# Three score blocks and four value blocks per visit of the tensor engine, in a fused attention, Fourier-mixing and FFN kernel

## The chip, the cores and the metric

The kernel runs on one core of one Trainium2 chip. The metric is the device time of one execution in microseconds (us), as the median over runs of the same program. TensorE is called PE below (its weight loads PEld), VectorE is DVE, ScalarE is ACT, GpSimd is POOL and SyncE is SP; "L509" is line 509 of the kernel before.

## The reference

Eight batches, twelve heads, 448 positions, 64 channels a head. The attention has no softmax: the scores are passed through a squared relu. Its output goes through two Fourier transforms whose real part is added to it, a layer norm, and an FFN with residual.

```python
scores = scale * np.matmul(q, k.transpose(0, 1, 3, 2))
attn = np.maximum(scores, 0.0) ** 2 / S
x = np.matmul(attn, v)                      # (B, H, S, D) -> (B, S, H * D)
X = np.fft.fft(np.fft.fft(x, axis=1), axis=2)
u = x + np.real(X)
un = (u - mean(u)) / np.sqrt(var(u) + 1e-06)
out = u + np.maximum(un @ w_ch1, 0.0) @ w_ch2
```

## The kernel before, in words

**Work per batch.** Two heads make one channel tile m of 128 channels, six tiles a batch (MC = 6). The 448 keys are cut in four blocks of 112. One score block (L509) is two matmuls, one per head: each contracts over 64 channels, on its own half of the array's rows, and writes 112 x 448 scores into one half of a two-bank PSUM tile psS. ACT takes the relu of such a tile into a bfloat16 tile sq (L541), DVE squares it in place (L536), and one value block (L525) is two matmuls, one per head, each into its own 64 partitions of a one-bank tile psT. Four value blocks accumulate in one psT; then DVE reads it twice (the two scaled copies into xT, L431 and L438) and makes the sum and the difference of its halves (L446, L447, and from the fourth tile on L456, L458). So a batch has 24 score blocks and 24 value blocks.

**The rest of a batch.** The folded tiles go through the channel transform (L815, 24 matmuls), are cast by ACT and DVE (L827), go through the sequence transform (L677, 8 matmuls), and become the rows u and the normalised rows un (L688 to L723 on ACT, DVE and POOL). u and un are stored to DRAM, and un comes back transposed as unT (L762). The FFN of a batch then has an up phase (L905: 24 groups of six matmuls, each group into one bank psF, relu into hT by ACT at L895, in the first batch every second one by DVE at L893) and a down phase (L940: groups of 24 matmuls into one bank psF, the residual added by DVE at L922). The FFNs take 384 and 512 rows in turn, so a matmul of the up phase streams 384 or 512 columns; a down phase has 144 or 192 matmuls of 384 columns.

**PSUM.** The eight banks are: two tiles psS of two banks each (tag S), two tiles psT of one bank (tag T) and two psF of one bank (tag F). psS also serves the transforms, psF the transposes of q and k in the first two batches (L409) and the warm-up matmuls (L959).

**What sets the order.** `Streams.run` writes the whole program in one pass on the host. Every part of the kernel is a generator that asks with `need(engine, duration, dependencies, buffers, ok)` for its next piece of work; the planner holds a clock per engine, from cost formulas (`mm`, `act`, `dve`, `dve2`, `SWITCH`, `LATENCY`), and gives the engine to the piece that can start first, and among equals to the lower rank. The lists `BS`, `BT` and `BF` hold the times at which the banks of the tags S, T and F come free by that clock. On the chip each engine then executes its instructions strictly in the written order and waits where an operand or a buffer isn't there. An attention of batch b may run ahead of the FFNs by `LEAD` only.

**A visit.** One turn of the loop in `attention` (L475 and after) is called a visit here: the score matmuls of G key blocks and, LAG visits later, the value matmuls of G key blocks, directly behind them in PE's order. G is 1 for the first two batches and 2 after that. The relus of the scores and the squares are asked for by the same generator, so the next visit is asked for when these have been placed. In the FFN likewise, the relu of a group is placed after the next group of matmuls was, by the same generator (`pend`).

**Other queues.** POOL issues the loads of q, k, v and of the weights, and SP the transposes and stores. The copies of q and k at L379 on DVE have one buffer each, which the transposing DMAs at L388 have to have read before the next copy.

## Time and profile before

| | before |
|---|---|
| median of three runs (lowest to highest) | 640.99 us (640.28 to 646.23) |
| the profiled execution: its time / its span from first to last instruction | 641.72 us / 639.8 us |
| busy PE / PEld | 618.9 us / 322.3 us |
| busy DVE / ACT / POOL | 332.6 us / 319.9 us / 126.7 us |
| granted clock of PE, mean over the span | 0.991 |
| DMA, mean | 131 GB/s |

The page of the profile gives busy time per engine, the chain of work that ended last, the costliest groups of instructions and the transfers. In a row of the groups, "x192 | 167.7, 916 | 135.0" means 192 instructions, busy 167.7 us together, 916 ns each on average, and 135.0 us in which the engine stood idle just before one of them. Busy time counts an instruction from its start to its modelled end, and neighbouring matmuls overlap; what a run of matmuls costs is therefore read from the chain of work, which gives the time from a piece's start to the next one's.

### The profile page before, as it was taken

To read this page: it belongs to the slowest core of one execution; us is meant where nothing else is said; L and a number is where in the kernel's file an instruction comes from. 1 tells how busy PE (TensorE), PEld (TensorE's weight loads), DVE (VectorE), ACT (ScalarE), POOL (GpSimd) and SP (SyncE) were. 2 spreads that over 40 slices of the span, in tenths; PEclk is the share of its full clock that TensorE was granted. 3 is DMA by queue.
4 is the path that set the end of the run, shared out by engine and by line. 5 is a ranking of instruction groups with operands and counts; after the bars stand their busy time and mean duration, and the time that the engine had idled before them with its cause. 6 is when DMAs were issued, how large, how long until landed. Compare 5 with 4: busy or idle time off the path is not lost.

```text
span 639.8 us, 10069 instructions
## 1 busy us (share of the span) xinstructions
PE 618.9 (97%) x3923; PEld 322.3 (50%) x3938; DVE 332.6 (52%) x763; ACT 319.9 (50%) x471; POOL 126.7 (20%) x176
## 2 busy tenths in 40 slices
PE   8997999899999999999999999999999999999997
PEld 5464445344544556444544556444544556554464
DVE  6866777676456435765366434765275435410011
ACT  6956752655575245754475245754575334404300
POOL 8342033311331103220241103311040002300000
PEclk9998999899999999999999999999999999999999
DMA  9999999688648658696547767698336213531021
GB/s 120 203 207 228 218 126 224 177 122 142 118 143 146 132 98 157 150 180 112 101 147 135 142 113 133 145 207 114 73 129 137 65 60 90 145 113 44 0 78 72
DMA packets 128688, 83.91 MB, mean 131 GB/s; under 512 B 79504, under 2 KB 116512, under 8 KB 128640
## 3 DMA queue, kind: packets, MB, share of 16 engines
q0 software_dynamic: 40512, 34.64, 33.7%
q1 hardware_dynamic: 88128, 48.63, 32.2%
q8 instruction: 31, 0.51, 0.4%
q14 instruction: 17, 0.14, 0.1%
HBM read 62.91 MB, written 27.60 MB: 141 GB/s over the span
## 4 chain that ended last, share of the span: by engine, by line
PE 80%; DVE 6%; ACT 6%; DMA 4%; issue 2%; SPq 1%; POOL 0%; DVEq 0%; ACTq 0%; POOLq 0%
PE psF L940 34%; PE psF L905 28%; PE psT L525 7%; PE psS L509 7%; ACT sq L541 3%; DMA unT<-nbot 2%; DMA qkT<-qkr 1%; PE psS L815 1%; DVE stats L709 1%; PE psS L677 1%; ACT un L723 1%; DVE u L698 1%; PE psS L506 1%; PE psS L791 1%; PE psF L959 1%
## 5 line engine op out<-in xcount | busy, mean ns | idle before, releaser
L541 ACT ACTIVATE sq<-psS 112x896 bf16<-112x896 f32 x192 | 167.7, 916 | 135.0 <-PE psS L509 134.7
L905 PE MATMUL psF<-unT,w 128*128 128x384 bf16 (+1 forms) x1137 | 229.0, 352 | 2.8 <-DVE hT L893 1.4
L940 PE MATMUL psF<-w,hT 128*128 128x384 bf16 x1344 | 229.4, 327 | 0.3 <-ACT hT L895 0.3
L940 PEld LDWEIGHTS <-hT 128*128 128x128 bf16 x1344 | 127.7, 98 | 100.4 <-issue 20.0
L905 PEld LDWEIGHTS <-w 128*128 128x128 bf16 x1152 | 109.2, 98 | 111.7 <-issue 15.9
L895 ACT ACTIVATE hT<-psF 128x512 bf16<-128x512 f32 (+1 forms) x180 | 98.3, 547 | 109.6 <-PE psF L905 106.9
L536 DVE TENSOR_TENSOR sq<-sq 112x896 bf16<-112x896 bf16 x192 | 113.3, 618 | 30.1 <-ACT sq L541 29.8
L922 DVE TENSOR_TENSOR o<-psF,o 128x384 f32<-128x384 f32 x56 | 31.2, 556 | 144.8 <-PE psF L940 144.7
L509 PE MATMUL psS<-qkT 64*112 64x448 bf16 x384 | 63.2, 380 | 6.0 <-ACT sq L541 6.0
L293 POOL DMA_DIRECT2D vn<-in_v_dram x24 | 17.4, 724 | 216.5 <-PE psT L525 216.5
L525 PE MATMUL psT<-sq,vn 112*64 112x448 bf16 x384 | 59.4, 371 | 0.2 <-DVE sq L536 0.2
L431 DVE TENSOR_SCALAR xT<-psT 128x224 bf16<-128x224 f32 x48 | 18.7, 390 | 53.4 <-PE psT L525 53.4
L509 PEld LDWEIGHTS <-qkT 64*112 64x112 bf16 x384 | 20.5, 125 | 41.8 <-issue 40.6
L697 POOL TENSOR_TENSOR u<-tp,xn 128x385 f32<-128x385 f32 (+1 forms) x14 | 14.5, 1033 | 116.0 <-DVE tp L688 109.8
L525 PEld LDWEIGHTS <-vn 112*64 112x64 bf16 x384 | 15.5, 108 | 33.6 <-issue 33.3
L723 ACT ACTIVATE un<-u,nmr,rstd 128x768 bf16<-128x768 f32 (+1 forms) x28 | 27.9, 1022 | 3.8 <-DVE nmr L718 3.7
L709 DVE BATCH_NORM_STATS2 stats<-u 128x6 f32<-128x384 f32 (+1 forms) x56 | 27.7, 534 | 0.0
L739 POOL DMA_INDIRECT ubot<-u,back x16 | 16.0, 1002 | 30.3 <-ACT sq L541 25.0
L739 POOL DMA_INDIRECT nbot<-un,back x15 | 14.5, 969 | 37.4 <-ACT un L723 32.4
L959 PE MATMUL psF<-warm 128*128 128x256 bf16 x114 | 18.9, 303 | 1.1 <-DVE warm L205 1.1
L827 DVE CAST pc<-psS 97x772 bf16<-97x772 f32 x8 | 8.2, 1030 | 20.8 <-PE psS L815 20.0
L438 DVE TENSOR_SCALAR xT<-psT 128x224 bf16<-128x224 f32 x47 | 18.1, 386 | 0.0
(122 smaller groups left out, 372.9 us busy)
## 6 DMA issues: line engine op xcount, KB each, us to landing
out_dram<-o SPq DMA_DIRECT2D x28, 384.0 KB
vn<-in_v_dram POOLq DMA_DIRECT2D x24, 224.0 KB, 5.2
qn<-in_q_dram POOLq DMA_DIRECT2D x21, 224.0 KB, 6.6
kn<-in_k_dram POOLq DMA_DIRECT2D x21, 224.0 KB, 8.3
w<-in_moe_w_ch_dram POOLq DMA_DIRECT2D x12, 384.0 KB, 13.5
w<-in_moe_w_ch_dram POOLq DMA_DIRECT2D x4, 1152.0 KB, 26.8
utop<-u SPq DMA_DIRECT2D x8, 384.0 KB
o<-utop SPq DMA_DIRECT2D x8, 384.0 KB
```

The source lines that it names most:

```text
L509: nc.tensor.matmul(sc[:R, h, 0:S].rearrange("k (c q) -> k c q", c=4), lhsT=kT[ps, m % 2, c, :], rhs=qT[ps, m % 2], start=True, stop=True)
L525: nc.tensor.matmul(av[h * Dh:(h + 1) * Dh, 0:S], lhsT=vn[:, c, h0 + h, :], rhs=sq[:, h, :], start=(c == 0), stop=(c == 3))
L536: nc.vector.tensor_tensor(r, r, r, op=ALU.mult)
L541: nc.scalar.activation(r, sc[:R, :, 0:S], AF.Relu)
L709: nc.vector.bn_stats(stats[:n, hf, :], u[:n, hf * (D // 2):(hf + 1) * (D // 2)])
L723: nc.scalar.activation(un[:n], u[:n], AF.Identity, bias=nmr[:n, i:i + 1], scale=rstd[:n, i:i + 1])
L739: nc.gpsimd.indirect_dma_start(out=bot, out_offset=bass.IndirectOffsetOnAxis(ap=back[ch][:s1 - s0], axis=0), in_=us[1][:s1 - s0], in_offse ...
L895: nc.scalar.activation(h[:, 0:N], ph[:, 0:N], AF.Relu)
L905: nc.tensor.matmul(ph[:, 0:N], lhsT=w1_sb[m][hf][:, jj * 128:(jj + 1) * 128], rhs=unT[:, m, 0:N], start=(m == 0), stop=(m == MC - 1))
L922: nc.vector.tensor_tensor(o[:, hs], pc[:, 0:D // 2], o[:, hs], op=ALU.add)
L940: nc.tensor.matmul(pc[:, 0:D // 2], lhsT=hT[j][:, c * 128:(c + 1) * 128], rhs=w2_sb[j // 6][:, j % 6, hs], start=(j == 0), stop=(j == JC - 1))
L959: nc.tensor.matmul(pw[:, 0:256], lhsT=warm[:, 0:128], rhs=warm, start=True, stop=True)
```

## The change

- **PSUM**: three tiles psS of two banks (tags S0 to S2) and two banks psF (F0, F1). The tag T is gone. A class `Banks` gives each tile a tag of its own and hands out the one that came free first. The values are collected in a bank psF; the warm-up matmuls and the last of the first batch's row tiles move from psF to psS.
- **A visit** issues the values first, all four key blocks of a channel tile at once (eight matmuls), once their squares belong to the scores issued a visit earlier (three visits earlier in the first batch and until the first FFN begins), and then the scores of three key blocks (six matmuls), one block in the early part. A visit may have only one of the two.
- **Streams of their own**: the relu of the scores (`squares`), each square (`square`), the relu of an FFN group (`relu`), the reloading of the residual (`reload`) and the residual add with its store (`add`) are generators that the planner places by themselves.
- **SBUF**: nine tiles sq instead of six, one tile xn instead of two.

```diff
+class Banks(Bufs):
+    def __init__(self, n, make):
+        super().__init__(n)
+        self.make, self.ids, self.tiles = make, [(0.0, i) for i in range(n)], {}
+    def take(self):
+        first = min(self.ids)
+        self.ids.remove(first)
+        t = self.make(first[1])
+        self.tiles[id(t)] = t, first[1]
+        return t
+    def give(self, t, when):
+        self.free.append(when)
+        self.ids.append((when, self.tiles.pop(id(t))[1]))
...
-        return psum.tile([128, 2, 512], FP32, name="psS", tag="S", bufs=2)
...
-    BS, BT, BF = Bufs(2), Bufs(2), Bufs(2)
+    BS = Banks(3, lambda i: psum.tile([128, 2, 512], FP32, name="psS", tag=f"S{i}", bufs=1))
+    BF = Banks(2, lambda i: psum.tile([128, 512], FP32, name="psF", tag=f"F{i}", bufs=1))
...
-    BSQ = Bufs(6)
+    NSQ = 9
+    BSQ = Bufs(NSQ)
...
-    BXN = Bufs(1)
+    BXN = Bufs(0)
...
-        BT.free.append(e1 - 2 * dve2(NS))
+        BF.give(av, e1 - 2 * dve2(NS))
...
-        G, LAG = (1, 3) if b < 2 else (2, 2)
-        NP = 4 * MC // G
...
+        while pa < NB:
+            few = b == 0 or progress[0] == 0.0
+            n = min(1 if few else 3, NB - p)
+            ma = pa // 4
+            lag = 3 if few else 1
+            old = fresh[-lag] if len(fresh) >= lag else 0
+            values = pa + 4 <= old if n else True
+            n = max(0, min(n, NSQ - (p - pa - 4 * values)))
+            values = values or not n
+            fresh.append(p + n)
             deps, bufs, dur = [], [], 0.0
+            if values:
+                deps += [sqs[i][1] for i in range(pa, pa + 4)]
+                bufs.append(BF)
...
+            if n:
+                deps += [turned_at[b][i // 8][i // 4 % 2] for i in (p, p + n - 1)]
+                bufs += [BS] * n
...
+            if scs:
+                sch.add(squares(scs, sqs), (0.2, 0.2))
             if av_end is not None:
                 yield from fold(b, ma, F, av, av_end)
+
+    def squares(scs, sqs):
+        for i, sc, t in scs:
+            e = yield need("ACT", act(2 * S) - 0.03, [t + LATENCY["PE"]], [BSQ])
+            r = sqs[i][0] = work.tile([R, 2, S], BF16, name="sq", tag="sq", bufs=NSQ)
+            nc.scalar.activation(r, sc[:R, :, 0:S], AF.Relu)
+            BS.give(sc, e + 0.1)
+            sch.add(square(r, e + LATENCY["ACT"], sqs[i][1]), (0.2, 0.2))
+
+    def square(r, t, done):
+        e = yield need("DVE", dve2(2 * S), [t])
+        nc.vector.tensor_tensor(r, r, r, op=ALU.mult)
+        done.t = e + LATENCY["DVE"]
...
-                if pend:
-                    yield from relu()
-                pend = (ph, e, j)
-                if j in (JC // 2, JC // 2 + 2):
-                    yield from reload()
...
+            sch.add(relu(ph, e, j), (0, 0))
+            if j in (JC // 2, JC // 2 + 2):
+                sch.add(reload(j // 2 - JC // 4), (4, 0))
...
-                        if jq == 0 and pend:
-                            yield from add()
-                    pend = (pc, e, c, half)
-            yield from add()
...
+                sch.add(add(pc, e, c, half), (0, 0))
```

**What moves in the order.** On PE, in the down phase of the third FFN (144 matmuls of 384 columns): psF are the FFN's groups, psS scores, psT values; of every run of like matmuls only the first row is shown. Before:

```order
L940 MATMUL psF_3302<-w2_0_811,hT_2936 128x384
...
L509 MATMUL psS_3334<-qkT_2690 112x448
...
L525 MATMUL psT_3340<-sq_3076,vn_2620 64x448
...
L940 MATMUL psF_3302<-w2_3_879,hT_3222 128x384
...
L509 MATMUL psS_3375<-qkT_2690 112x448
...
L525 MATMUL psT_3340<-sq_3316,vn_2620 64x448
...
L940 MATMUL psF_3359<-w2_2_856,hT_3126 128x384
```

The same place with the change, where a visit takes the values (L524) ahead of the scores (L542):

```order
L959 MATMUL psF_3405<-w2_0_798,hT_2956 128x384
...
L524 MATMUL psF_3455<-sq_3349,vn_2824 64x448
...
L542 MATMUL psS_3464<-qkT_2923 112x448
...
L959 MATMUL psF_3447<-w2_1_822,hT_3091 128x384
...
L542 MATMUL psS_3529<-qkT_2923 112x448
...
L959 MATMUL psF_3508<-w2_3_849,hT_3285 128x384
```

Before, the runs have 18, 4, 4, 18, 4, 4 and 12 matmuls; with the change 30, 8, 6, 36, 6 and 36. The runs have become longer and fewer, and the second visit shown has no values.

Counted over the whole of PE's order from the first FFN group on, these are the runs of like matmuls that lie between others:

| runs on PE from the first FFN group on | before | with the change |
|---|---|---|
| of scores (322 matmuls) | 89 | 54 |
| of values (328 matmuls) | 91 | 41 |
| of FFN matmuls, up and down (2496) | 122 | 91 |

With the change 26 of the score runs of six lie in up phases and 27 in down phases, and 21 of the value runs in up phases and 20 in down phases. Ahead of the first FFN group there are 62 score and 56 value matmuls in both orders, in 31 and 27 runs before, in 28 and 7 with the change, and 142 and 152 warm-up matmuls.

On ACT, in the up phase of the third FFN, sq is the relu of one score block and hT that of one FFN group. Before:

```order
L541 ACTIVATE sq_2925<-psS_2913 112x896
L895 ACTIVATE hT_2936<-psF_2906 128x384
L541 ACTIVATE sq_2938<-psS_2916 112x896
L895 ACTIVATE hT_2956<-psF_2929 128x384
L895 ACTIVATE hT_2965<-psF_2945 128x384
L895 ACTIVATE hT_2974<-psF_2958 128x384
```

With the change, at the sixteenth group of the same up phase:

```order
L562 ACTIVATE sq_3238<-psS_3213 112x896
L920 ACTIVATE hT_3248<-psF_3224 128x384
L562 ACTIVATE sq_3254<-psS_3216 112x896
L920 ACTIVATE hT_3264<-psF_3241 128x384
L920 ACTIVATE hT_3266<-psF_3256 128x384
L562 ACTIVATE sq_3276<-psS_3219 112x896
```

A visit in an up phase now puts three relus of scores among those of the FFN's groups.

On PE in the up phase of the third FFN, the bank of the values. Before, psT lies beside psF:

```order
L905 MATMUL psF_2929<-unT_2515,w1_0_0_341 128x384
...
L525 MATMUL psT_2976<-sq_2874,vn_2194 64x448
...
L905 MATMUL psF_2984<-unT_2515,w1_0_0_341 128x384
...
L525 MATMUL psT_2976<-sq_2925,vn_2194 64x448
...
L905 MATMUL psF_3028<-unT_2515,w1_0_0_341 128x384
```

With the change the values take one of the two psF:

```order
L943 MATMUL psF_3224<-unT_2631,w1_0_1_427 128x384
...
L524 MATMUL psF_3290<-sq_3023,vn_2564 64x448
...
L542 MATMUL psS_3299<-qkT_2734 112x448
...
L943 MATMUL psF_3323<-unT_2631,w1_0_1_427 128x384
...
L524 MATMUL psF_3363<-sq_3254,vn_2564 64x448
```

From the values' first matmul until DVE has read their bank, the FFN has one bank of the two.

More of the change, by code (lines that the diff above doesn't have):

```diff
@@ L564, in first_rows @@
         n = s1 - s0
-        BP = [BS, BT, BS, BF][2 * ch + i]
+        BP = BF if (ch, i) == (0, 1) else BS
         e = yield need("PE", 8 * mm(D // 2) + 6 * 0.06, [pcs[0][1], pcs[1][1]] + x_ready[0],
-                       [BP] * (1 + i))
-        if i:
-            pu = [(psF if ch else psT)() for _ in range(2)]
-        else:
-            pu = psS()
-            pu = [pu[:, 0], pu[:, 1]]
+                       [BP] * (2 if BP is BF else 1))
+        if BP is BF:
+            pu = held = [BF.take() for _ in range(2)]
+        else:
+            held = [BS.take()]
+            pu = [held[0][:, 0], held[0][:, 1]]
         for hf in range(2):
@@ L630, in first_rows @@
         e1, e2 = ends
-        BP.free += [e1, e2] if i else [max(e1, e2)]
+        for t, e in zip(held, (e1, e2) if BP is BF else (max(e1, e2),)):
+            BP.give(t, e)
         first_us[ch][i] = u, max(e1, e2) + LATENCY["ACT"], max(e1, e2)
@@ L958, in warming @@
             e = yield need("PE", 0.12 if e > 5.0 else 0.23, [e + gap])
-            nc.tensor.matmul(pw[:, 0:256], lhsT=warm[:, 0:128], rhs=warm, start=True, stop=True)
-        BF.free.append(e)
+            nc.tensor.matmul(pw[:, 0, 0:256], lhsT=warm[:, 0:128], rhs=warm, start=True, stop=True)
+        BS.give(pw, e)
     LEAD = 1.9
```

269 lines of the change are left out of this document (120 added, 149 removed).

## The prediction

> **What bounds the kernel now.** I first read the busy times on the page and the stage in which all FFNs but the last run.
>
> ```profile
> PE 618.9 (97%) x3923; PEld 322.3 (50%) x3938; DVE 332.6 (52%) x763; ACT 319.9 (50%) x471; POOL 126.7 (20%) x176
> 127.00:546.00 419.00, 414.39 (x2533) 209.99 (x2545) 231.09 (x530) 221.04 (x328) 76.69 (x88) 1.00 0.63 127
> ```
>
> In the second row the columns are length, then busy time of PE, PEld, DVE, ACT and POOL, granted clock, DMA share and GB/s. PE is busy for 414.4 of 419 us at full clock, DVE and ACT for little more than half of it. PE is the bound, but its busy time doesn't say what it does with the time, since overlapping matmuls are counted to their modelled ends. So I went to the waits of PE next, from 70 us on, where the columns are total, times and longest.
>
> ```profile
> PE psS L509 <- ACT sq L541: 5.8, 12, 1.7
> PE psF L905 <- DVE hT L893: 1.4, 3, 0.9
> PE psF L905 <- ACT hT L895: 0.7, 2, 0.5
> PE psF L940 <- ACT hT L895: 0.3, 2, 0.2
> ```
>
> Together 8.2 us. Waiting is not where much can be had. What is left is the chain of work, which shows what a run of matmuls costs from its start to the next run's: start, length, what. The first three rows are from the stage with one block a visit, the others from the stage with two.
>
> ```profile
> 66.80 0.33 PE psS L509 x2
> 67.13 0.31 PE psT L525 x2
> 67.44 1.08 PE psF L905 x6
> ...
> 259.41 3.09 PE psF L940 x18
> 262.50 0.52 PE psS L509 x4
> 263.01 0.50 PE psT L525 x4
> ...
> 267.56 2.06 PE psF L940 x12
> ...
> 280.90 4.01 PE psF L940 x24
> ...
> 296.28 5.29 PE psF L905 x24
> ```
>
> Two score matmuls take 0.33 us and four take 0.52: a block adds 0.19, so the run itself costs 0.33 - 0.19 = 0.14 beside its matmuls. Values: 0.31 and 0.50, again 0.19 a block and 0.12 for the run. FFN matmuls of 384 columns: 1.08, 2.06 and 4.01 us for 6, 12 and 24, so 0.98 for six and 0.10 for the run. The price belongs to the change of kind and not to the semaphore waits: each value block in a run has its own wait on DVE, and the second still adds only 0.19.
>
> **Part 1: fewer runs.** From the first FFN group on, the order has 35 score runs less (89 to 54), 50 value runs less (91 to 41) and 31 FFN runs less (122 to 91). That removes 35 x 0.14 + 50 x 0.12 + 31 x 0.10 = 4.9 + 6.0 + 3.1 = 14.0 us, with the same matmuls. A score run of six then takes 0.14 + 3 x 0.19 = 0.71 us, a value run of eight 0.12 + 4 x 0.19 = 0.88. Nothing hides this: PE is the bound there. Ahead of the first FFN group the value runs fall from 27 to 7, but there the gaps are filled with warm-up matmuls (142 before, 152 after), so a shorter run only makes room for them; I take nothing.
>
> The Trainium skill gives this price a cause and a smaller size. By "TensorEngine Tiling (Array Packing)", Key Properties, changing the tiling mode drains the array, and scores (half the rows), values (half the columns) and FFN (the whole array) are three modes; by "TensorE: Matmul & The Clock Gate", Step-by-step, draining takes some 128 cycles, which is an estimate of 0.053 us at 2.4 GHz. By that the 116 runs less would give 6.2 us, and the sum below 636.8 us instead of 629.0. The rows show 0.10 to 0.14 us for a run, so the sum goes by them.
>
> **Part 2: waits for a score tile.** Twelve waits make the 5.8 us quoted above. They lie where two visits follow one another with little between them:
>
> ```profile
> 199.19 3.34 ACT L541 ACTIVATE sq<-psS 112x896 bf16<-112x896 f32 x4 [1.35 <-PE psS L509]
> 200.16 0.40 PE L509 MATMUL psS<-qkT 64*112 64x448 bf16 x2 [0.32 <-ACT sq L541]
> 200.96 0.40 PE L509 MATMUL psS<-qkT 64*112 64x448 bf16 x2 [0.41 <-ACT sq L541]
> ```
>
> Four relus take ACT 3.34 us and PE asks for the third and fourth tile too early, 0.73 us in each batch. With the change nearly every pair of score runs has at least 18 FFN matmuls, 3 us, between them; I found one place where only six and a value run (0.98 + 0.10 + 0.88 us) stand between. Three relus take 2.75 us by the first row of part 3. I take 4 of the 5.8 us as gone; the bounds are 0 and 5.8.
>
> **Part 3: three relus among those of the FFN.** The durations, as count, busy, mean ns, and idle before:
>
> ```profile
> L541 ACT ACTIVATE sq<-psS 112x896 bf16<-112x896 f32 x136 | 117.9, 915 | 121.0 <-PE psS L509 121.0
> L895 ACT ACTIVATE hT<-psF 128x512 bf16<-128x512 f32 x92 | 55.0, 598 | 71.7 <-PE psF L905 69.6 <-issue 2.1
> L895 ACT ACTIVATE hT<-psF 128x384 bf16<-128x384 f32 x72 | 35.1, 490 | 25.6 <-PE psF L905 25.0 <-issue 0.5
> ```
>
> In an up phase the FFN has two banks; the bank of one group has to be read while PE makes the next, 0.98 us at 384 columns and 5.29 / 4 = 1.32 us at 512. A group's relu that comes just after a score relu has begun ends 0.92 + 0.49 = 1.41 us after its matmuls, or 0.92 + 0.60 = 1.52: late by 0.43 or 0.20 us. In the long run ACT has the time: a visit with three scores, four values and 18 FFN matmuls of 384 columns is 0.71 + 0.88 + 3.04 = 4.63 us of PE and 3 x 0.92 + 3 x 0.49 = 4.23 of ACT. But three relus in a row come close to that. The order has 26 such visits in up phases, where before most score runs lay in down phases. Bounds: 0 if the longer runs of PE cover it, and two late groups a visit at 384 columns, 26 x 0.86 = 22 us, above. I take 0.2 us a visit, near the lower end because the separate streams put an FFN relu between the score relus as soon as it is there: +5 us.
>
> **Part 4: the values' bank.** The two reads of a value tile, and what may stand ahead of them on DVE:
>
> ```profile
> L431 DVE TENSOR_SCALAR xT<-psT 128x224 bf16<-128x224 f32 x35 | 13.7, 392 | 48.0 <-PE psT L525 48.0
> L438 DVE TENSOR_SCALAR xT<-psT 128x224 bf16<-128x224 f32 x35 | 13.5, 385 | 0.0
> L698 DVE TENSOR_TENSOR u<-tp,xn 128x383 f32<-128x383 f32 x6 | 7.6, 1270 | 0.0
> ```
>
> Before, they held a bank psT that nobody else wanted. Now they hold one of the FFN's two, for 0.78 us behind the last value matmul. PE makes an FFN group in the other bank meanwhile, 0.98 or 1.32 us, and in most visits 0.71 us of scores too, so the usual cost is nothing. If the longest neighbour, 1.27 us, stands ahead, the bank comes free after 2.05 us, and PE has waited 0 to 1.07 us. In a down phase a bank is filled for 4 us and the cover is mostly longer. Queued behind the waiting FFN matmul is all of PE. Bounds: 0, and 21 x 1.07 = 22 us. I take 0.05 us for each of the 21 value runs in up phases, since the neighbour of 1.27 us occurs once or twice a batch: +1 us.
>
> **Part 5: the rest.** One tile xn instead of two: it is written again only by the first value tile of the next batch, in the order at least 54 FFN matmuls of the up phase, 9 to 12 us, after the last sequence transform that leads to its reads; hidden by these. SP and POOL have the same number of rows to within one. At the start, the scores of the first batch are still one block a visit, and the first FFN group needs unT, which needs the fold of the last values. These values stand a little later in the order, and the row tiles have one tile psS more; the waits that this concerns are
>
> ```profile
> 54.51 0.34 PE L644 MATMUL psS<-rev,un 128*128 128x63 bf16 x6 [1.76 <-ACT unT L651]
> 58.06 0.64 PE L644 MATMUL psS<-ident,un 96*128 96x96 bf16 x6 [1.65 <-ACT u L629]
> ```
>
> so 3.4 us could be gained, and as much lost if the last tile comes that much later. I take 0, between these.
>
> **Sum.** The profiled execution took 641.7 us, 1.9 us more than its span and 0.7 us above the median. 641.7 - 14.0 - 4 + 5 + 1 = 629.7 us, and 0.7 less beside the median: **629.0 us**, 1.9% under 640.99.
>
> **The rivals.** *The gain is given back by ACT and DVE.* Parts 3 and 4 come at 0.25 us for each of the 47 runs of scores or values in up phases, 12 us, and the start loses 1 us: 641.0 - 14.0 - 4 + 12 + 1 = 636.0, within 1%. For it speaks that a visit in an up phase fills 4.23 of 4.63 us on ACT, against it that PE has few waits in the present up phases, which have part of the score runs too. By the Trainium skill, "TensorEngine Tiling (Array Packing)", PSUM Bottleneck, reading PSUM may become the bound once tiling has made the array faster; no row here shows it yet.
>
> *More is gained.* The streams of their own make part 3 free, and the waits of part 2 go entirely: 641.0 - 14.0 - 5.8 = 621.2, with 1 us of other waits 622. The 52% of busy DVE and 50% of ACT speak for it; the 4.23 us against it.
>
> *Slower: the values' bank hangs on DVE's queue.* DVE executes in order, and it already waits there for transfers:
>
> ```profile
> DVE qkr L379 <- DMA qkT<-qkr: 18.7, 12, 3.2
> ```
>
> These 12 waits, up to 3.2 us, cost PE little while the values had a bank of their own. If such a copy stands ahead of the reads at L431, one of the FFN's banks is held as long, and PE with it. All of the 18.7 us passed on, and the neighbour of 1.27 us ahead of every second read in an up phase (10 x 1.07 = 11 us), is 641.0 - 18 + 18.7 + 11 = 652.7. It decides the sign from 18 us on, the 14 and 4 gained, and is slower by over 1% from 24.4. Against it: most of the 41 value runs have at least one FFN group or a score run as cover behind them.
>
> *The runs don't get cheaper.* If a score run of three tiles paid its 0.14 us for each tile, the 4.9 us would be gone and the time 634; the 0.52 us of a run with two tiles speaks against it. This lies inside the forecast's chance.
>
> **How the numbers follow.** A measurement here tells about 1% from no change. Forecast, with its variants from 624 to 634.5: 0.58. More gained: 0.15. Given back: 0.17. Slower: 0.10. So faster by over 1% (below 634.6) 0.73, within 1% 0.17, slower 0.10. The range runs from 620, under the second rival, to 638, above the first; it leaves out most of the slower case and the ends.
>
> **What would show it.** Right: in the chain of the profile after, score runs of six at 0.71 us, value runs of eight at 0.88, FFN runs of 36 at 5.95; PE's waits on sq under 3 us, its waits for hT of ACT in up phases at 3 to 8 us, for the xT reads under 2 us. The first FFN group begins at 67 us, give or take 3. Wrong: a wait of PE's L943 or L959 on DVE's reads of over 10 us in total, or of L943 on ACT of over 12, or runs that cost more than their matmuls by 0.2 us and more.

## The result, and the profile after

The changed kernel takes 623.79 us in the median of four runs (620.43 to 625.59), the kernel before 642.12 us in four runs beside them (640.28 to 646.23). The ratio is 0.970, with an interval of 0.963 to 0.977. The prediction was 629.0 us with a range of 620 to 638. The ratios in this document are those on record with each run; they leave out three executions, two of run 3 and one of run 4, that lay over 1.5% above the fastest of their kernel, and are not the quotients of the medians shown. The profiled execution of the changed kernel took 620.43 us with a span of 618.6; it is the fastest of its four runs, and a second profile of the same kernel (run 9) has a span of 626.5.

The first row is from the page of after (busy time by engine), the second from the busy times by stretch, in the same stage as before the change: length, then PE, PEld, DVE, ACT, POOL, granted clock, DMA share, GB/s.

```profile
PE 600.6 (97%) x3948; PEld 326.7 (53%) x3948; DVE 329.8 (53%) x763; ACT 315.7 (51%) x471; POOL 127.1 (21%) x176
127.00:546.00 419.00, 417.80 (x2622) 224.78 (x2621) 230.35 (x533) 220.83 (x334) 81.10 (x92) 1.00 0.67 136
```

PE is still the bound, DVE and ACT hardly work more or less. PE is busy for 417.8 of the 419 us and was for 414.4, so some 3 us of idle time went. In the same 419 us the trace now has 2622 matmuls, and had 2533 (2621 and 2545 weight loads). So most of the gain is not idle time that was filled: the same busy time holds more matmuls.

The chain of work of after, from the third and fourth FFN (start, length, what):

```profile
245.60 0.88 PE psF L524 x8
246.48 0.70 PE psS L542 x6
247.19 3.03 PE psF L943 x18
...
251.85 1.08 PE psF L943 x6
...
259.39 5.96 PE psF L959 x36
...
293.67 1.40 PE psF L943 x6
...
304.87 5.29 PE psF L943 x24
```

Eight values take 0.88 us, six scores 0.70, 36 FFN matmuls 5.96, and six still 1.08 (1.40 at 512 columns). The runs are longer and pay their price once, as worked out ahead.

The waits of PE in after from 70 us on (total, times, longest):

```profile
PE psF L943 <- DVE xT L450: 1.9, 1, 1.9
PE psF L943 <- ACT hT L920: 0.7, 2, 0.5
PE psF L959 <- DVE xT L450: 0.6, 1, 0.6
PE psF L524 <- ACT hT L920: 0.5, 1, 0.5
PE psF L943 <- DMA unT<-nbot: 0.4, 1, 0.4
PE psF L524 <- DVE sq L568: 0.2, 1, 0.2
```

They add up to 4.3 us, and were 8.2. The waits of scores for a tile, 5.8 us before, are gone altogether. New are the waits of FFN groups for the bank of the values (L450 is the second read of it), 1.9 and 0.6 us, each once. The larger one is the mechanism of the slower rival, seen in the timeline of after (start, length, instruction, in brackets the idle time before it and its releaser):

```profile
98.02 0.43 DVE L390 COPY qkr<-kn 112x1024 bf16<-112x1024 bf16 x1 [3.09 <-DMA kn<-in_k_dram]
98.36 0.38 DVE L443 TENSOR_SCALAR xT<-psF 128x224 bf16<-128x224 f32 x1
98.66 0.39 DVE L450 TENSOR_SCALAR xT<-psF 128x224 bf16<-128x224 f32 x1
...
99.11 1.15 PE L943 MATMUL psF<-unT,w 128*128 128x384 bf16 x6 [1.92 <-DVE xT L450]
```

A copy of k waits 3.09 us for its load; behind it in DVE's queue stand the two reads of the values' bank, and behind these the next FFN group on PE. It happened once. The other one, 0.64 us at 122.50 us, has no copy ahead of its reads, but work on DVE of 1.01 us (L734) and 0.21 us (L735). After 140.5 us there is no wait of PE over 0.15 us until 520 us.

**Where the 21.2 us between the two spans lie.** A stretch here runs from the first matmul of one up phase to that of another. Up to the first up phase after gains 0.85 us (67.37 to 66.52), from the first to the third 8.2 us (161.34 to 153.17), from the third to the seventh 10.9 us, and behind that 1.3 us. The third to the seventh, four whole batches, is the steady part; the busy times of that stretch, of before

```profile
228.71:519.25 290.54, 286.87 (x1754) 145.64 (x1760) 159.33 (x364) 154.00 (x228) 53.07 (x60) 1.00 0.63 128
```

and of after

```profile
219.69:499.33 279.64, 279.54 (x1763) 149.63 (x1760) 157.48 (x365) 151.75 (x229) 53.03 (x60) 1.00 0.66 133
```

show the same work in 290.54 and in 279.64 us. After's 279.64 came out to within 0.01 us in four profiled executions (this one and runs 9, 10 and 11), so the stretch can separate causes where the whole time can't; it is called *the stretch* below.

### The profile page after: what moved, and what is told of

It reads as the page before. It is cut to its first block, busy times and chain, and to the rows that moved or that the text cites. A ratio compares the mean times of both kernels' runs of the same rounds, so it can differ in the third digit from the quotient of the medians.

```text
span 618.6 us, 10034 instructions
## 1 busy us (share of the span) xinstructions
PE 600.6 (97%) x3948; PEld 326.7 (53%) x3948; DVE 329.8 (53%) x763; ACT 315.7 (51%) x471; POOL 127.1 (21%) x176
## 4 chain that ended last, share of the span: by engine, by line
PE 74%; DMA 9%; ACT 6%; DVE 5%; issue 3%; POOL 1%; SPq 0%; POOLq 0%; DVEq 0%; ACTq 0%
PE psF L959 32%; PE psF L943 27%; PE psS L542 5%; PE psF L524 5%; DMA ubot<-u,back 4%; ACT sq L562 2%; PE psS L840 2%; DMA kn<-in_k_dram 2%; DMA qkT<-qkr 1%; DVE stats L734 1%; DMA nbot<-un,back 1%; DMA unT<-nbot 1%; PE psS L702 1%; ACT un L748 1%; DVE u L723 1%
## 5 line engine op out<-in xcount | busy, mean ns | idle before, releaser
L562 ACT ACTIVATE sq<-psS 112x896 bf16<-112x896 f32 x192 | 165.1, 917 | 132.1 <-PE psS L542 131.8
L943 PE MATMUL psF<-unT,w 128*128 128x512 bf16 (+1 forms) x1152 | 229.0, 353 | 3.2 <-DVE xT L450 1.9
L959 PE MATMUL psF<-w,hT 128*128 128x384 bf16 x1344 | 224.2, 326 | 0.6 <-DVE xT L450 0.6
L568 DVE TENSOR_TENSOR sq<-sq 112x896 bf16<-112x896 bf16 x192 | 115.6, 619 | 51.4 <-ACT sq L562 50.0
L443 DVE TENSOR_SCALAR xT<-psF 128x224 bf16<-128x224 f32 x48 | 18.7, 389 | 74.7 <-PE psF L524 70.3
L542 PE MATMUL psS<-qkT 64*112 64x448 bf16 x384 | 53.8, 369 | 1.6 <-ACT sq L562 1.0
L524 PE MATMUL psF<-sq,vn 112*64 112x448 bf16 x384 | 45.6, 358 | 1.1 <-ACT hT L920 0.5
L542 PEld LDWEIGHTS <-qkT 64*112 64x112 bf16 x384 | 20.9, 125 | 30.6 <-issue 26.5
L524 PEld LDWEIGHTS <-vn 112*64 112x64 bf16 x384 | 18.3, 109 | 23.4 <-issue 15.9
L734 DVE BATCH_NORM_STATS2 stats<-u 128x6 f32<-128x384 f32 (+1 forms) x56 | 28.2, 539 | 0.0
L975 PE MATMUL psS<-warm 128*128 128x256 bf16 x124 | 20.1, 292 | 1.1 <-DVE warm L215 1.1
L450 DVE TENSOR_SCALAR xT<-psF 128x224 bf16<-128x224 f32 x47 | 18.1, 385 | 0.0
L303 POOL DMA_DIRECT2D qn<-in_q_dram x21 | 15.6, 741 | 6.8 <-PE psF L421 6.1
## 6 DMA issues: line engine op xcount, KB each, us to landing
w<-in_moe_w_ch_dram POOLq DMA_DIRECT2D x12, 384.0 KB, 14.4
```

The source lines that it names most:

```text
L303: nc.gpsimd.dma_start(out=t, in_=src[b, hs].rearrange("h (p j) d -> p h (j d)", j=4))
L524: nc.tensor.matmul(av[h * Dh:(h + 1) * Dh, 0:S], lhsT=vn[:, c, h0 + h, :], rhs=sq[:, h, :], start=(c == 0), stop=(c == 3))
L542: nc.tensor.matmul(sc[:R, h, 0:S].rearrange("k (c q) -> k c q", c=4), lhsT=kT[ps, m % 2, c, :], rhs=qT[ps, m % 2], start=True, stop=True)
L562: nc.scalar.activation(r, sc[:R, :, 0:S], AF.Relu)
L568: nc.vector.tensor_tensor(r, r, r, op=ALU.mult)
L734: nc.vector.bn_stats(stats[:n, hf, :], u[:n, hf * (D // 2):(hf + 1) * (D // 2)])
```

## The experiments

The theory on trial, called the run theory, is the prediction's Part 1 and 2: the gain is what PE saves by starting fewer runs, and the waits for a score tile. Its rivals: the order that the streams of their own give the relus and squares makes the gain; or the longer runs and the third tile only give the load of ACT, DVE and the queues another place. The medians are all from chips on which the kernel before ran too: its median there was 642.49 us beside runs 1 to 4, 645.76 beside runs 5 to 8 and 643.93 beside runs 9 to 11. The stretch is from the profiled execution.

| run | what | median, us | ratio to before | the stretch, us |
|---|---|---|---|---|
| | before | 642.12 | | 290.54 |
| | after | 623.79 | 0.970 (0.963 to 0.977) | 279.64 |
| 1 | after, values and scores of a visit alternate | 644.69 | 1.004 (1.000 to 1.007) | 294.50 |
| 2 | after, two score blocks a visit | 643.07 | 0.998 (0.994 to 1.001) | 284.93 |
| 3 | before, values of all four blocks in one run | 638.98 | 0.995 (0.990 to 1.000) | 287.06 |
| 4 | before, with the streams of their own | 642.82 | 0.996 (0.991 to 1.000) | 288.19 |
| 5 | after, relus and squares of scores inline | 672.72 | 1.044 (1.037 to 1.050) | 301.91 |
| 6 | after, relu, reload and add of the FFN inline | 635.70 | 0.988 (0.981 to 0.995) | 285.04 |
| 7 | after, values' bank held longer | 634.06 | 0.980 (0.973 to 0.988) | 283.17 |
| 8 | run 2 with two buffers for the copies | 646.09 | 1.004 (1.000 to 1.008) | 289.67 |
| 9 | after once more | 624.75 | 0.968 (0.963 to 0.973) | 279.64 |
| 10 | after with two buffers for the copies | 625.46 | 0.968 (0.962 to 0.974) | 279.64 |
| 11 | after, copies planned later | 621.83 | 0.964 (0.959 to 0.969) | 279.64 |

**Run 1: the same visits, cut into short runs.** A visit that has both issues one value block, one score block, and so on in turn. The tiles, the streams and the rest stay.

```diff
-                for c in range(4):
-                    sq = sqs.pop(pa + c)[0]
+                v0 = pa
+                def value(c):
+                    sq = sqs.pop(v0 + c)[0]
...
+                mixed = n == 3
+                for c in range(1 if mixed else 4):
+                    value(c)
...
                 scs.append((i, sc, e - SWITCH - (p + n - 1 - i) * mm(S)))
+                if values and mixed:
+                    value(1 + i - p)
```

> The kernel with the change, but in each of the 33 visits that have both values and three score blocks, PE's matmuls are issued in turn: two value matmuls, two score matmuls, and so on. Nothing else in any engine's order moves, and the same work is done. That makes 66 score runs and 99 value runs more. Run theory (each run of like matmuls pays 0.14 us for scores and 0.12 for values): 66 x 0.14 + 99 x 0.12 = 21 us more, 645 us instead of 623.8; between the first matmul of the third and of the seventh up phase, 279.64 us after the change, 20 such visits are 40 x 0.14 + 60 x 0.12 = 12.8 us, so 292.4. Placement theory (the gain comes from the relus and adds being placed by themselves, and the runs cost little): both stay within 3 us of the kernel with the change.

The whole gain is gone: 644.69 us. The chain of this run, in a down phase:

```profile
266.90 0.31 PE psF L526 x2
267.21 0.33 PE psS L548 x2
267.85 0.33 PE psS L548 x2
...
275.08 0.70 PE psS L548 x6
```

Two values and two scores take 0.31 and 0.33 us again, the same as in before with one block a visit, and a run of six in a visit without values 0.70. The stretch has 72 score and 84 value runs here, and 32 and 24 in after: 40 x 0.14 + 60 x 0.12 = 12.8 us, and PE waits 1.6 us in it for DVE's residual adds. That is 14.4 of the 14.86 us that the stretch is longer. This run has all streams, all tiles and all buffers of the change, and in its trace ACT, DVE, POOL and SP execute the same operations in the same order as in after; it lacks the long runs alone. By the estimate of 0.053 us a run that the prediction worked out from the Trainium skill ("TensorEngine Tiling (Array Packing)", Key Properties, and "TensorE: Matmul & The Clock Gate", Step-by-step), these 100 runs would have cost 5.3 us. The trace bears out that a change of kind has a price, and that it is more than twice that; whether a drain is what is paid, no run here shows.

**Run 2: two score blocks a visit instead of three**, values as in the change.

```diff
-            n = min(1 if few else 3, NB - p)
+            n = min(1 if few else 2, NB - p)
```

> The kernel with the change, but with two score blocks a visit instead of three; the three score tiles, the values of four blocks and the separate streams stay. PE's order has 81 score runs instead of 54 and 103 FFN runs instead of 79. Run theory: 27 x 0.14 + 24 x 0.10 = 6.2 us more, 630 us; between the third and the seventh up phase 16 x 0.14 + 14 x 0.10 + 2 x 0.1 = 3.8 us more, 283.5. ACT theory (three relus in a row held the FFN's banks up): the stretch gets shorter or stays, since only two relus come together.

In the stretch it went about as the run theory wanted, +5.3 us: 16 score runs and 14 FFN runs more are 2.2 + 1.4, waits 0.7, and 1.0 us is left over (the channel transform is in six pieces there, in after in four). The median of 643.07 was a miss by 13 us, and nearly all of it lies ahead of the third up phase, which begins at 236.03 us, and in the two profiles of the change at 219.69 and (run 9) 227.53. The timeline of this run shows the two largest waits there:

```profile
102.00 0.43 DVE L390 COPY qkr<-kn 112x1024 bf16<-112x1024 bf16 x1 [5.05 <-DMA qkT<-qkr]
102.34 0.55 DVE L918 TENSOR_SCALAR hT<-psF 128x384 bf16<-128x384 f32 x1
102.94 1.71 PE L524 MATMUL psF<-sq,vn 112*64 112x448 bf16 x8 [4.63 <-DVE hT L918]
...
154.83 2.72 PE L943 MATMUL psF<-unT,w 128*128 128x512 bf16 x6 [5.69 <-issue]
```

A copy waits 5.05 us for the transposing DMA that has to read its only buffer; the read of an FFN bank stands behind it, and the values on PE wait 4.63 us for that bank. At 154.83 the second FFN starts 5.69 us late; the profile names no releaser for this wait, but at the same place runs 4 and 8 wait for the transposed input of that FFN. So two score blocks a visit cost 5.3 us in four batches, mostly by their runs, and some 10 us more lie in two waits of the first 160 us, of which the first is shown to go back to a transfer. With the visits the order on all other engines changes too, so these 10 us are those of this order and not the price of two blocks as such.

**Run 3: before with the values in long runs only.** From the third batch on every second visit issues eight value matmuls, in a bank psT of their own; the scores stay four a visit with two tiles, no streams.

```diff
-            if p >= LAG:
+            values = p >= LAG and (G == 1 or (p - LAG) % 2 == 1)
+            if values:
...
+                VN = G
+                if G == 2:
+                    ca, VN = 0, 4
...
-                dur += G * mm(S) + SWITCH
+                dur += VN * mm(S) + SWITCH
...
-                for c in range(ca, ca + G):
+                for c in range(ca, ca + VN):
...
-    BSQ = Bufs(6)
+    BSQ = Bufs(9)
```

> The kernel before, from the third batch on with the values of four key blocks in one run every second visit, in their own banks psT; nine tiles sq and one xn to make this possible; everything else as before (two score tiles, two scores a visit, relus and adds placed by the same generators). PE's order has 55 value runs instead of 91 and 100 FFN runs instead of 108. Run theory: 36 x 0.12 + 8 x 0.10 + 2 x 0.14 = 5.4 us less than before, 636; between the third and the seventh up phase, 290.54 us before, 24 x 0.12 + 6 x 0.10 + 2 x 0.14 = 3.8 less, 286.8. Bank theory (taking the values out of banks of their own cost the change something): this kernel gains more for its runs than that, by 2 us or more in the stretch.

The stretch is 3.5 us shorter than before. It has 24 value runs, 6 FFN runs and 2 score runs less: 24 x 0.12 + 6 x 0.10 + 2 x 0.14 = 3.8 us. The waits for a score tile remain; from 70 us on PE waits for

```profile
PE psS L520 <- ACT sq L552: 5.8, 9, 1.7
```

5.8 us for a tile, as before. So the long value runs alone don't take these waits away. What does can be read from PE's order in the traces. In the stretch of before all of these waits lie at four places, one a batch, where two score runs follow one another with no FFN matmul between them, and run 3 has these four places too. After has at least 18 FFN matmuls between any two score runs of the stretch.

**Run 4: before with the streams of their own**, for relus, squares, the reload and the add; tiles and visits as before.

```diff
+            if scs:
+                sch.add(squares([(p * G + i, sc, e - dur * 0.5) for i, sc in enumerate(scs)], sqs), (0.2, 0.2))
...
+            sch.add(relu(ph, e, j), (0, 0))
+            if j in (JC // 2, JC // 2 + 2):
+                sch.add(reload(j // 2 - JC // 4), (4, 0))
...
+                sch.add(add(pc, e, c, half), (0, 0))
```

> The kernel before with the relus of scores, the squares, the FFN relus, the reloads and the residual adds as streams of their own; tiles, banks and the size of a visit as before. PE's order has the same 89 score runs, 89 value runs instead of 91 and 110 FFN runs instead of 108. Run theory: within 2 us of before; between the third and the seventh up phase 290.5 less up to 2.9, the waits of 0.73 us in each of its four batches for a score tile, plus 4 x 0.10: 288 to 291. Placement theory: most of the change's 10.9 us in this stretch comes here already, 283 or less.

The whole time is that of before, or 0.9% less at the most by the interval. The stretch wins 2.4 us, part of it because the waits for a score tile give way to shorter ones for a transfer. With two tiles psS only, there is no wait for a score tile: at least 12 FFN matmuls stand between any two score runs of this stretch. So in the stretch these waits end with the distance of the score runs, and with two blocks a visit two tiles are enough for that. The waits of PE from 70 us on:

```profile
PE psF L924 <- DMA unT<-nbot: 5.6, 1, 5.6
PE psT L525 <- DVE sq L550: 4.2, 1, 4.2
PE psS L509 <- DMA qkT<-qkr: 1.8, 2, 1.0
```

The first two lie at 151.28 and 103.38 us, in the first two FFNs, and lose more than the stretch wins. At 103.38 a copy of k that waits 5.58 us for a transposing DMA stands on DVE ahead of the square, so such a copy holds PE even where the values have banks of their own. The streams alone make 2.4 of the 10.9 us in the stretch and nothing that shows in the whole time. That rival falls, but only in this form, as the next run shows.

**Run 5: the change without the streams of relus and squares.** The visit places them itself, ahead of the next visit.

```diff
-                sch.add(squares(scs, sqs), (0.2, 0.2))
+                yield from squares(scs, sqs)
...
-            sch.add(square(r, e + LATENCY["ACT"], sqs[i][1]), (0.2, 0.2))
+            yield from square(r, e + LATENCY["ACT"], sqs[i][1])
```

> The kernel with the change, but the relus and squares of a visit's three score blocks are again placed by the attention's own generator, in turn, before its next visit is asked for. PE's order has 55 score, 42 value and 79 FFN runs, as with the change. Run theory: within 2 us of 279.6 in the stretch from the third to the seventh up phase. If their own stream was needed: the next visit is asked for late, the order on ACT puts three relus and squares ahead of what else is ready, and PE waits for squares or for hT: 282 or more.

672.72 us, 4.4% slower than before, with the same number of runs on PE to within one of a kind. The waits of PE from the third to the seventh up phase:

```profile
PE psF L959 <- DVE o L928: 8.1, 12, 0.7
PE psF L943 <- ACT hT L920: 4.2, 6, 0.8
PE psF L943 <- DVE o L928: 3.4, 5, 0.7
PE psF L959 <- ACT hT L920: 1.4, 2, 0.7
```

One of the five in the third row ends where the stretch begins and so lies ahead of it. Without it, and with 0.6 and 0.4 us of smaller ones, they are 17.3 of the 22.3 us that the stretch is longer than after's: 24 times in four batches PE waits up to 0.8 us for a relu or an add of the FFN. One such place (start, length, instruction):

```profile
286.08 0.62 DVE L568 TENSOR_TENSOR sq<-sq 112x896 bf16<-112x896 bf16 x1 [2.92 <-ACT sq L562]
286.62 0.55 DVE L928 TENSOR_TENSOR o<-psF,o 128x384 f32<-128x384 f32 x1
287.23 3.08 PE L959 MATMUL psF<-w,hT 128*128 128x384 bf16 x18 [0.68 <-DVE o L928]
```

A square stands on DVE directly ahead of the add at all of the waits for an add, and two relus of scores in a row stand on ACT ahead of the relu at six of the eight waits for hT. The latter is what Part 3 of the prediction feared; the squares ahead of the adds it didn't name. The streams of their own keep both away: needed with the long visits, worth at most 2.4 us of the stretch without. The rest of the 49 us by which this run is longer than after lies mostly ahead of the third up phase, which begins at 250.06 us.

**Run 6: the change without the streams of the FFN.** The relu of a group is placed behind the matmuls of the next again, the reload and the add inline.

```diff
-            sch.add(relu(ph, e, j), (0, 0))
+            if pend:
+                yield from relu(*pend)
+            pend = ph, e, j
...
-                sch.add(add(pc, e, c, half), (0, 0))
+                    if jq == 0 and pend:
+                        yield from add(*pend)
+                pend = pc, e, c, half
```

> The kernel with the change, but the FFN relus, reloads and residual adds are again placed by the FFN's own generator, each after the next group of matmuls has been placed. PE's order has the same 54 score, 41 value and 78 FFN runs. If the streams of the FFN were needed to keep its banks free beside the values: PE waits for hT or for the bank, 0.2 to 0.4 us in each of the 47 runs in up phases, 5 to 12 us more in all, and the stretch from the third to the seventh up phase 283 to 287 instead of 279.6. If the runs alone make the gain: within 2 us of 279.6 there.

635.70 us: of the gain of 3.0% there remain 1.2. The stretch is 5.4 us longer than after's; in it PE waits four times for

```profile
PE psF L944 <- DVE xT L450: 3.2, 4, 0.8
```

the values' bank, 0.8 us in each up phase. The other 2.2 us of the stretch have no wait over 0.15 us in the trace.

**Run 7: the values' bank held longer.** From the third batch on DVE reads it twice more, into a tile nobody uses (work that the reference doesn't ask for).

```diff
+        for _ in range(2 if b > 1 else 0):
+            nc.vector.tensor_scalar(hold, at[:, 0:R // 2], 1.0 / (64.0 * S), None, op0=ALU.mult)
         BF.give(av, e1 - 2 * dve2(NS))
```

> The kernel with the change, but from the third batch on DVE reads each value tile two more times (the copy of L443 into a tile nobody reads), 0.39 us each, before the bank is given back, and the planner's costs don't know of it. PE's order is the same. If the cover behind the values (an FFN group of 0.98 to 1.32 us, in most visits 0.71 us of scores too) is longer than the hold of 0.78 us by enough, as the stretch without any wait of PE says: 0 to 2 us more in the stretch from the third to the seventh up phase. If the bank is near its limit: the 12 value runs in up phases of that stretch wait 0.5 us each and the others a little, 6 us or more, as waits of PE on these reads.

The stretch is 3.5 us longer, between what the two theories wanted. The two reads add 0.31 and 0.40 us by the chain,

```profile
236.28 0.31 DVE hold L453
...
236.61 0.40 DVE hold L453
```

which is 24 times 0.71 or 17 us in four batches, and PE is 3.5 us later. The waits of PE in the stretch are 1.8 us,

```profile
PE psF L946 <- DVE o L931: 0.9, 2, 0.4
PE psF L946 <- DVE hold L453: 0.9, 2, 0.4
```

and 1.7 us are not to be found in it. So a fifth of the added time comes through: the bank has cover most of the time, but not to spare. Whether the 0.78 us of the change itself cost anything in the stretch can't be read from this run; in after no such wait is seen there.

**Run 8: run 2, its copies with two buffers** (and two tiles sq less, for the space), against the loss in the first 160 us.

```diff
-    QN, QR = 2, 1
+    QN, QR = 2, 2
...
-    NSQ = 9
+    NSQ = 7
```

> The kernel with two score blocks a visit (e4) came out at 643.1 us, 19 above the change, where the runs explain 6. Its stretch from the third to the seventh up phase was 284.9, as the runs say (283.5); the rest was lost before, at three places up to 155 us, where DVE's copies of q and k waited 5.05, 2.80 and 6.00 us for the transposing DMAs, and PE 4.63, 1.25 and 5.69 us behind them. This kernel is e4 with two buffers for each of these copies (and seven tiles sq instead of nine, to make room), so that a copy needn't wait for the transpose just before it. Queue theory (DVE's queue, held by such a copy, holds the values' bank or the relus of the FFN): the waits of 4.63 and 1.25 go, the 5.69 at the second up phase perhaps too; 631 to 638 us, the third up phase begins at 224 to 230 us instead of 236.0. Load theory (the transfers themselves are late there, whatever DVE waits for): PE waits at the same places for as long, the third up phase begins at 234 to 237.

Run 2's wait of 4.63 us, and another of 1.25 us that stood behind a copy in the same way, are gone, and the time isn't better: 646.09. The waits from 70 us on:

```profile
PE psF L943 <- DMA unT<-nbot: 7.7, 1, 7.7
PE psF L943 <- ACT hT L920: 5.4, 8, 0.9
```

The first one stands at 148.82 us: the second FFN waits for its transposed input. The copy's buffer was one link of the chain of transfers at the start of the program; the next link takes its place. The third up phase begins at 233.18 us, where the queue theory wanted 224 to 230 and the load theory 234 to 237. In the stretch there are new waits for hT (3.0 us) and xT (2.2) as well; whether the two buffers or the two tiles sq less brought them, this run doesn't tell apart.

**Run 9: the changed kernel once more**, without an edit.

> The kernel with the change as it is, beside the two that follow on the same chip: 620 to 626 us, a stretch of 279.6 us from the third to the seventh up phase, and the two waits of PE on DVE's reads of a value tile (1.92 us at 99 us, 0.64 at 122).

624.75 us, and a profiled execution with a span of 626.5, 7.9 us above the first. The stretch is the same 279.64, and the difference is in the early part: the third up phase begins at 227.53 us. The timeline:

```profile
104.68 0.43 DVE L390 COPY qkr<-kn 112x1024 bf16<-112x1024 bf16 x1 [7.23 <-DMA qkT<-qkr]
...
105.77 1.46 PE L943 MATMUL psF<-unT,w 128*128 128x384 bf16 x4 [6.06 <-DVE xT L450]
```

The same place as the 1.92 us of the first profile, with a copy that waited 7.23 us. Most of what the values' bank costs lies at this one place, and it differs by 4 us from one execution to the other.

**Run 10: the change with two buffers for the copies**, as in run 8.

> The kernel with the change with two buffers for DVE's copies of q and k, and seven tiles sq instead of nine. PE's order has nearly the same runs (54, 41 and 77). If the copies' waits for the transposes cost the change something: 1 to 3 us less than the kernel with the change. If the wait of 1.92 us, which is for the load of k, is all: no difference beyond 1 us. The stretch from the third to the seventh up phase 279.2 to 279.7 in both cases, unless nine tiles are needed: then longer by waits for squares.

625.46 us, no difference from run 9 on the same chip. The bank's wait is gone, and in its place from 70 us on stand

```profile
PE psS L542 <- DMA qkT<-qkr: 3.3, 1, 3.3
PE psF L943 <- DVE sq L568: 2.1, 1, 2.1
```

The scores on PE now wait themselves for the transposing DMA of q and k. The stretch shows besides that seven tiles sq do as well as nine once the program runs steadily.

**Run 11: the copies later in DVE's order.** The planner is told that the loads of q and k of the third batch land 5 us later, so it places their copies behind the reads of the values. With them up to 200 us some transposes, reloads and loads also come at another place in the queues of SP and POOL, and some runs in PE's order, so the run changes more than the copies.

```diff
-            ready[i][x].t = sch.dma(e, GRP, 360e3, "sw") + (0.0, 3.0, 7.0)[min(b, 2)]
+            ready[i][x].t = sch.dma(e, GRP, 360e3, "sw") + (0.0, 3.0, 12.0 if b == 2 else 7.0)[min(b, 2)]
```

> The kernel with the change, but the planner takes the loads of the third batch's q and k to land 5 us later than it did, so that it places DVE's copies of them later, behind the reads of a value tile that they held up at 98 us. Queue theory (the 1.92 us of PE are the copy of k waiting 3.09 us for its load, ahead of the reads): this wait is gone, and the time 1 to 3 us less, if nothing later takes its place. If the second up phase then waits for its unT (it began at 140.54 us with 0.39 us of wait): no gain in the time, and that wait longer.

621.83 us, the best of all, and the ratio 0.964 (0.959 to 0.969) overlaps that of run 9, 0.968 (0.963 to 0.973): a gain of 3 us is possible and not proven. The wait for the bank is gone, and of the early part is left

```profile
PE psF L943 <- DMA unT<-nbot: 2.4, 1, 2.4
```

2.4 us at the start of the second FFN.

## Why the prediction was right, and where its steps were off

The direction, the bound and the mechanism held. The forecast gain was 12.0 us and the measured one is 18.3, because two of the terms, Parts 2 and 3, were sized wrongly, by some 3 and 5 us. Both errors went the same way; Part 4, too low by 1.5 us in one profile and by 5 in the other, went against them, and that the forecast came within 5 us of 623.8 is in part luck.

- **Part 1, fewer runs (14.0 us).** Right in kind and size. S6, V8 and F36 were said to take 0.71, 0.88 and 5.95 us, and take 0.70, 0.88 and 5.96. Run 1 put 100 runs back in the stretch and moved nothing on the other engines, and it became 14.86 us longer, where the prices give 12.8 and its waits 1.6. One count was off by little: an up and the following down phase were taken as two runs, but are of the same kind and cost no change (30 matmuls of a down phase behind six of an up phase take 4.88 us at 252.93 us in the chain of after, five times 0.98), so it is 29 FFN runs less and not 31, and the term 13.8.
- **Part 2, waits for a score tile (4 taken of 5.8).** Right in kind, as the waits went where FFN matmuls stand between the score runs (runs 3 and 4), and mis-sized: the whole 5.8 went, and there is a little more behind them. Two of the twelve waits, 1.73 and 0.41 us at 121.72 us, don't fit the reading of two visits in a row: 12 FFN matmuls stand ahead of them. At each of the four places of the stretch before, PE takes 2.02 us from the start of the value run ahead to that of the value run behind, instead of 0.50 + 0.52 us. Of these 1.00 us the profile counts 0.73 as waits; the other 0.27 a batch come on top. For the stretch this gives 16 x 0.14 + 24 x 0.12 + 16 x 0.10 = 6.7 us of runs, 2.9 of waits for a tile, 0.3 of waits for hT and 4 x 0.27 = 1.1 of stopped runs: 11.0, of 10.9 measured. No run tried the 1.1 apart.
- **Part 3, three relus among the FFN's (+5 taken).** Mis-sized: the waits for hT of ACT are 0.7 us as before, and 0.5 for the values, so next to nothing. The step that failed is the 0.2 us a visit. It was taken from a visit that fills 4.23 of 4.63 us on ACT, though the same paragraph named the cover, the streams of their own. Run 5 took that cover away from the relus and squares of the scores and paid 17.3 us of waits in four batches: 5.5 for hT, and 10.8 for DVE's residual adds, which the step had not thought of. The chain of after shows what the streams do:

```profile
240.69 0.37 ACT hT L920
241.07 0.81 ACT sq L562
241.88 0.38 ACT hT L920
242.26 0.81 ACT sq L562
```

  A group's relu stands ahead of each relu of scores here, and no two relus of scores follow one another.
- **Part 4, the values' bank (+1 taken).** 2.5 us in the first profile, 6.1 in the second; in the stretch none. The 0.05 us for each of 21 runs was the wrong shape: it is not a little everywhere but one large wait, 1.9 and 6.1 us, where a copy that waits for a transfer stands ahead of the reads. A neighbour on DVE of about 1 us, which Part 4 took as the usual cause, cost 0.64 us once.
- **Part 5, the start (0).** The first FFN begins at 66.52 us instead of 67.37, and at 69.04 in run 9: no difference that can be told from that between two executions.

For the whole program: runs 13.8, waits of PE from 70 us on 8.2 - 4.3 = 3.9, start 0.85 and the stopped runs of the stretch 1.1 are 19.7 of the 21.2 us between the spans. The other 1.5 us lie outside the stretch and have no cause here.

**The rivals.** *More is gained*, at 622 us, was nearest: it had Part 2 whole and Part 3 free, as it came. *Given back by ACT and DVE* did not happen with the change; without its streams it did, wholly in run 5 and in part in run 6. *Slower, the bank hangs on DVE's queue*, is a true mechanism at a tenth to a third of its price of 18.7 us (1.9 and 6.1 us). The copies of q and k wait less with the change. Those of q don't wait at all in after; the group of k's (count, busy, mean ns, idle before and its releasers):

```profile
L390 DVE COPY qkr<-kn 112x1024 bf16<-112x1024 bf16 x18 | 7.9, 441 | 5.5 <-DMA kn<-in_k_dram 3.1 <-DMA qkT<-qkr 2.4
```

Waits of 18.7 us became 5.5 us in this profile and 8.9 in run 9: the rival took the copies' waits over from the order before, and in the new order they stand elsewhere. *The runs don't get cheaper* is out by the 0.70 us of six scores.

**What stays open.** Why the transfers of the first 160 us come as late as they do in runs 2, 4 and 8, and by how much one execution's differ from another's; the runs show only which buffer or queue passes the delay on. What PE waited for in the 5.69 us of run 2. And whether run 11 is faster than the change by itself, and by which of the moves in its order.

## What to carry to other kernels

Read the price of a change of kind from runs of different length in the chain of work, and count the runs: a tensor engine that is 99% busy can still lose 3% to the order of its matmuls. Here longer runs needed more tiles to write to and readers that are placed apart from them. Take the change's parts off one at a time, since a part that is worth little alone can be what keeps the others' gain. Before a bank is shared, look at what stands ahead of its reader in the same queue, transfers above all.

## What the hardware showed beside that

**A long wait of PE costs more than it shows.** The busy times by stretch of run 2 (length, PE, PEld, DVE, ACT, POOL, granted clock, DMA share, GB/s):

```profile
102.00:112.00 10.00, 9.06 (x60) 5.28 (x59) 5.76 (x13) 3.14 (x4) 2.08 (x3) 0.83 0.97 132
```

Around the wait of 4.63 us the granted clock falls to 0.83 over these 10 us, from 1.00 in the 10 us ahead, and the eight values took 1.71 us. In the timeline of after eight values take

```profile
138.50 0.95 PE L524 MATMUL psF<-sq,vn 112*64 112x448 bf16 x8
```

Behind the 5.69 us at 154.83 six FFN matmuls of 512 columns took 2.72 us, where the timeline of after has 1.47 (at 293.60 us); the granted clock is 0.88 from 155 to 165 us. Behind the 1.92 us of after nothing changed: six matmuls in 1.15 us. This agrees with the Trainium skill, "TensorE: Matmul & The Clock Gate", "What's actually happening", by which one idle window of about 3.4 us brings the clock down to half. So these waits of 4.63 and 5.69 us cost about a microsecond more than they show: 1.71 - 0.95 = 0.76 and 2.72 - 1.47 = 1.25.
